# A causal convolution feeding a maxout layer: the band held still, the input moving, and DMA transposes in place of repack moves

## The chip, the cores and the metric

The kernel runs on one core of a Trainium2 chip. The metric is the device time of one execution in microseconds (us); it was measured three times before the change: 473.76, 473.94 and 474.82 us, median 473.94 us. The profile shown below is of one further execution, with a span of 472.8 us.

## The reference

The input `x` has 8 sequences of 4160 tokens with 192 channels. The channels form 8 heads of 24. Each head has a causal filter over 7 tokens, whose weights are a softmax. The 33280 filtered tokens go through a layer that takes the largest of three projections to 768 and projects that back to 192.

```python
w = exp(weight - max) / sum                      # 8 heads x 7 taps
x_pad = 6 zero tokens ahead of each sequence
y[b, s, h, :] = sum_k w[h, k] * x_pad[b, s + k, h, :]
h   = max(y @ w1, y @ w2, y @ w3)                # 192 -> 768
out = h @ w_out                                  # 768 -> 192, float32
```

The kernel uses max(a, b, c) = c + max(max(a - c, 0), b - c): it multiplies `y` by w1 - w3 and w2 - w3 and adds `y @ (w3 @ w_out)` at the end.

## The kernel before

The tokens are worked in 65 blocks of 512: 64 blocks out of the sequences, and one (block 58 in the order of work) of the last 64 tokens of all eight. A block goes through these parts:

- `load_x`: a DMA on SyncE's queue brings the tokens as float32, token by partition, in five chunks of 112 tokens that overlap by six and more.
- `cast_x`: GpSimd turns them into float16.
- `conv`: TensorE. A 112-by-32 piece of `x` is the stationary operand, a band matrix with the filter of one head is the moving one. The result in PSUM has channels as partitions and tokens as columns. As 24 channels don't fill 32 columns of the array, each head has a slot of 32.
- `evac`: ScalarE and VectorE copy the result to SBUF as float16.
- `repack`: six DMAs close the gaps between the slots, so that 64 channels lie in 64 partitions, three times (`yd`).
- `double`: one DMA copies the lower 64 partitions of `yd` to the upper 64, as TensorE works with two row groups of 64 at a time.
- `l1`: for each of six strips of 128 hidden units, TensorE computes the two differences into the PSUM tiles `lp` and `lq`; ScalarE takes max(lp, 0), VectorE the maximum with `lq`, to give `h`.
- `st2`: TensorE multiplies `h` by `w_out` and `y` by w3 @ w_out into `po`; ScalarE and VectorE add the two halves, and a DMA on GpSimd's queue stores the result.

The first four blocks have a convolution of their own (`conv_dense`), which the change leaves as it is.

```python
P, NBLK, HALF, PAD, GRP, NHEAD = 128, 512, 64, 6, 24, 8
SLOTS = ((0, 1, 2, 3), (6, 7, 4, 5))

def cast_x(t):
    ...
    for (rl, q0, q1) in parts:
        nc.gpsimd.tensor_copy(out=v[0:rl, q0:q1, :], in_=xf[0:rl, q0:q1, :])

def conv(t, pools=((psw, "w"), (psw, "w"))):
    G = [pool.tile([P, NBLK], FP32, ...) for i, (pool, tag) in enumerate(pools)]
    for (q, b, row_lo, rlen, lo, hi, cc) in chunks_of[t]:      # 5 chunks of up to 103 tokens
        for i in range(2):
            for g in range(4):
                h = SLOTS[i][g]
                cb = q * D + GRP * h + EDGE * (g % 2)
                nc.tensor.matmul(
                    G[i][32 * g:32 * g + 32, lo:hi],
                    lhsT=x16[0:rlen, cb:cb + 32],
                    rhs=band[0:rlen, h, cc:cc + hi - lo],
                    start=True, stop=True, tile_position=(0, 32 * g))

def evac(t, i, copy=nc.scalar.copy):
    copy(out=slots[t][:, i, :], in_=convs[t][i][:])

def repack(t):
    for n, (half, s0, c, r0, rows) in enumerate(pieces):       # 6 pieces
        (nc.sync, nc.gpsimd)[n % 2].dma_start(out=yd[r0:r0 + rows, c, :],
                                              in_=slots[t][s0:s0 + rows, half, :])

def double(t):
    nc.sync.dma_start(out=dense[t][HALF:P, :, :], in_=dense[t][0:HALF, :, :])

def make_m(i):                                                 # w3 @ w_out, once
    ...
            for e in range(2):
                nc.tensor.matmul(ps[HALF * e:HALF * (e + 1), :], lhsT=w3t[:, j, P:D],
                                 rhs=wo[:, j, :], start=(j == 0), stop=(j == NJ - 1))

def l1(t, j, pools=((psp, "p"), (psq, "q"))):
    for c in range(NC):                                        # 3
        for i in range(2):
            row = slice(HALF * i, HALF * (i + 1))
            nc.tensor.matmul(ps[i][:, 0:N], lhsT=wd[row, c, P * j:P * (j + 1)],
                             rhs=y[row, c, 0:N], start=(c == 0), stop=(c == NC - 1))
    nc.scalar.activation(out=r, in_=ps[0], func=AF.Relu)
    nc.vector.tensor_max(out=hs[t][:, j, 0:N], in0=r, in1=ps[1])
...
for t in range(2, NB):            # the steady state, t > 4
    load_x(t + 6)
    double(t + 2)
    cast_x(t + 5)
    l1(t, 0)
    if t % 2 == 0:                # the convolutions of two blocks together
        conv(t + 3); conv(t + 4)  # then evac: twice ScalarE, twice VectorE
    repack(t + 3)
    st2(t - 1, 0, NJ)
    for j in range(1, NJ):
        l1(t, j)
        st2(t - 1, j, NJ)
    store(t - 1)
```

Of the kernel before, what the change touches and what calls it, by code (L numbers as in the profile page):

```python
# [9 lines left out]
FP32 = mybir.dt.float32  # L10
FP16 = mybir.dt.float16
# [3 lines left out]
P = 128  # L15
KW = 7
PAD = KW - 1
NHEAD = 8
GRP = 24
BAND_W = 128 + PAD  # L20
NBLK = 512
CHK = 103
HALF = P // 2
# [4 lines left out]
def kernel(  # L28
# [12 lines left out]
    nc = tc.nc  # L41
    ctx.enter_context(tc.manual_schedule())

    B, SEQ, D = x.shape
# [6 lines left out]
    blocks = []  # L51
# [4 lines left out]
    segs, off = [], 0  # L56
# [25 lines left out]
                            o_lo - (row_lo - S)))  # L82
        return res

    chunks_of = [conv_chunks(blk) for blk in blocks]
    NQ = len(chunks_of[0])

    const = ctx.enter_context(tc.tile_pool(name="const", bufs=1))
    xap = ctx.enter_context(tc.tile_pool(name="xap", bufs=1))
    xbp = ctx.enter_context(tc.tile_pool(name="xbp", bufs=1))  # L90
    xfp = ctx.enter_context(tc.tile_pool(name="xfp", bufs=6))
    ysp = ctx.enter_context(tc.tile_pool(name="ysp", bufs=4))
    ydp = ctx.enter_context(tc.tile_pool(name="ydp", bufs=6))
    rp = ctx.enter_context(tc.tile_pool(name="rp", bufs=4))
    hp = ctx.enter_context(tc.tile_pool(name="hp", bufs=2))
# [4 lines left out]
    psq = ctx.enter_context(tc.tile_pool(name="psq", bufs=2, space=bass.MemoryType.PSUM))  # L100
    psw = ctx.enter_context(tc.tile_pool(name="psw", bufs=4, space=bass.MemoryType.PSUM))

    NDENSE = 4

    SLOTS = ((0, 1, 2, 3), (6, 7, 4, 5))
    EDGE = 32 - GRP
    xin = {}  # L110
    nlast = len(chunks_of[ENDS])
    x16s = [const.tile([P, NQ * D + 2 * EDGE], FP16, name=f"x16_{i}") for i in range(4)]
    x16z = const.tile([P, nlast * D + 2 * EDGE], FP16, name="x16_z")

    def load_x(t, eng=nc.sync):
        if not 0 <= t < NB:
            return
        chunks = chunks_of[t]
        n = len(chunks)
        pool, tag = (xfp, "xf") if t > 1 else ((xap, "xa"), (xbp, "xb"))[t]  # L120
        xf = (pool.tile([P, NQ, D], FP32, tag=tag, name=f"xf_{t}") if n <= NQ else
              const.tile([P, n, D], FP32, name=f"xf_{t}"))
        parts = []
        i, n = 0, len(chunks)
        row = [c[1] * SEQ + c[2] for c in chunks]
        while i < n:
            k = i
            while (k + 1 < n and chunks[k + 1][3] == chunks[i][3]
                   and row[k + 1] - row[k] == row[i + 1] - row[i]):
                k += 1  # L130
            step = row[i + 1] - row[i] if k > i else 0
            rlen = chunks[i][3]
            src = bass.AP(tensor=x.tensor, offset=row[i] * D,
                          ap=[[D, rlen], [step * D, k - i + 1], [1, D]])
            eng.dma_start(out=xf[0:rlen, i:k + 1, :], in_=src)
            if parts and parts[-1][0] == rlen:
                parts[-1] = (rlen, parts[-1][1], k + 1)
            else:
                parts.append((rlen, i, k + 1))
            i = k + 1  # L140
        xin[t] = [xf, None, parts]

    def cast_x(t):
        if not 0 <= t < NB:
            return
        xf, _, parts = xin[t]
        n = len(chunks_of[t])
        x16 = x16s[t % 4] if n <= NQ else x16z
        v = x16[:, EDGE:EDGE + n * D].rearrange("p (q d) -> p q d", d=D)
        for (rl, q0, q1) in parts:  # L150
            nc.gpsimd.tensor_copy(out=v[0:rl, q0:q1, :], in_=xf[0:rl, q0:q1, :])  # L151
        xin[t][1] = x16

    NC, NSLOT, CYC = D // HALF, D // 32, 96
    assert all(len(chunks_of[t]) == NQ for t in range(NDENSE))
    xz = {t: [const.tile([P, NQ, D], FP16, name=f"xz_{t}_{v}") for v in range(2)] for t in range(2)}
    xz[2], xz[3] = xz[0], xz[1]

# [38 lines left out]
    make_identity(nc, ident[:])  # L199
    ident16 = const.tile([P, P], FP16)  # L200
    nc.gpsimd.tensor_copy(out=ident16[:], in_=ident[:])
    for x16 in x16s + [x16z]:
        w = x16.shape[1] - EDGE
        nc.gpsimd.memset(x16[:, 0:EDGE], 0.0)
        nc.gpsimd.memset(x16[:, w:w + EDGE], 0.0)

    idle = const.tile([P, NBLK], FP16)
    nc.vector.memset(idle[:], 0.0)  # L208
    def keep_warm(n, pool=psw, tag="w"):
# [74 lines left out]
        nc.scalar.copy(out=m16[:, i, :], in_=ps[:])  # L284


    slots, dense, hs, outs, halves, convs, done = {}, {}, {}, {}, {}, {}, {}

    def conv(t, pools=((psw, "w"), (psw, "w"))):
        if t >= NB:  # L290
            return
        G = [pool.tile([P, NBLK], FP32, tag=tag, name=f"G{i}_{t}") for i, (pool, tag) in enumerate(pools)]
        x16 = xin[t][1]
        for (q, b, row_lo, rlen, lo, hi, cc) in chunks_of[t]:
            for i in range(2):
                for g in range(4):
                    h = SLOTS[i][g]
                    cb = q * D + GRP * h + EDGE * (g % 2)
                    nc.tensor.matmul(  # L299
                        G[i][32 * g:32 * g + 32, lo:hi],  # L300
                        lhsT=x16[0:rlen, cb:cb + 32],
                        rhs=band[0:rlen, h, cc:cc + hi - lo],
                        start=True, stop=True, tile_position=(0, 32 * g))
        slots[t] = ysp.tile([P, 2, NBLK], FP16, tag="ys", name=f"ys_{t}")
        convs[t] = G
        xin.pop(t)

    def conv_dense(t, copies):

# [31 lines left out]
    def evac(t, i, copy=nc.scalar.copy):  # L341
        if t >= NB:
            return
        copy(out=slots[t][:, i, :], in_=convs[t][i][:])  # L344


    pieces = ((0, 8, 0, 0, 48), (0, 72, 0, 48, 16), (0, 88, 1, 0, 32),
              (1, 72, 1, 32, 32), (1, 104, 2, 0, 16), (1, 8, 2, 16, 48))

    def repack(t):  # L350


        if t >= NB:
            return
        yd = dense[t] = ydp.tile([P, NC, NBLK], FP16, tag="yd", name=f"yd_{t}")
        for n, (half, s0, c, r0, rows) in enumerate(pieces):
            (nc.sync, nc.gpsimd)[n % 2].dma_start(out=yd[r0:r0 + rows, c, :],  # L357
                                                  in_=slots[t][s0:s0 + rows, half, :])

    def double(t):  # L360

        if NDENSE <= t < NB:
            nc.sync.dma_start(out=dense[t][HALF:P, :, :], in_=dense[t][0:HALF, :, :])

    def l1(t, j, pools=((psp, "p"), (psq, "q"))):


        N, y = blkN[t], dense[t]
        ps = [pool.tile([P, NBLK], FP32, tag=tag, name=f"l{tag}{i}_{t}_{j}")
              for i, (pool, tag) in enumerate(pools)]  # L370
        for c in range(NC):
            for i in range(2):
                row = slice(HALF * i, HALF * (i + 1))
                nc.tensor.matmul(ps[i][:, 0:N], lhsT=wd[row, c, P * j:P * (j + 1)],  # L374
                                 rhs=y[row, c, 0:N],
                                 start=(c == 0), stop=(c == NC - 1))
        r = rp.tile([P, NBLK], FP16, tag="r", name=f"r_{t}_{j}")
        nc.scalar.activation(out=r[:, 0:N], in_=ps[0][:, 0:N], func=AF.Relu)  # L378
        nc.vector.tensor_max(out=hs[t][:, j, 0:N], in0=r[:, 0:N], in1=ps[1][:, 0:N])  # L379

    def st2(t, u, NU):
# [2 lines left out]

        if t < 0:
            return
        hT, y = hs[t], dense[t]
        if u == 0:
            todo = [[], []]
            for s in range(4):  # L390
                tok = slice(P * s, P * (s + 1))
                for i in range(2):
                    row = slice(HALF * i, HALF * (i + 1))
                    mm = [(y[row, i, tok], m16[row, 0, :])]
                    if s % 2 == i:
                        mm.append((y[row, 2, tok], m16[row, 1, :]))
                    hh = [(hT[row, j, P * s:P * (s + 1)], wo[row, j, :]) for j in range(NJ)]
                    mm = hh + mm if t == 0 else mm + hh
                    todo[i] += [(s, n == 0, n == len(mm) - 1, m) for n, m in enumerate(mm)]
            if t == NB - 1:  # L400

                for i in range(2):
                    k = [sum(e[0] < s for e in todo[i]) for s in range(5)]
                    lot = [todo[i][k[s]:k[s + 1]] for s in range(4)]
                    todo[i] = lot[0][:-1] + lot[1][:-1] + lot[0][-1:] + lot[1][-1:] + lot[2] + lot[3]
            halves[t] = (todo, {})
# [99 lines left out]

    convs_at = {2: (4,), 3: (5, 6)}
    doubles_at = {2: (), 3: (4,), 4: (5, 6)}  # L510
    for t in range(2, NB):
        if t > 4:
# [9 lines left out]
        if t == 2:  # L522
            conv_dense(3, (nc.scalar.copy, nc.vector.tensor_copy, nc.scalar.copy))
            cross_dma(3)
            load_x(7)
        us = convs_at.get(t, (t + 3, t + 4) if t % 2 == 0 else ())
        for n, u in enumerate(us):
            conv(u, PQ if n or t == 2 else ((psw, "w"), (psw, "w")))
        for u in us:
            evac(u, 0)  # L530
        for u in us[::-1]:
            evac(u, 1, nc.vector.tensor_copy)
        if t == 2:
            repack(4)
            load_x(8)
            cast_x(5)
            cast_x(6)
        elif t == 3:
            repack(5)
            repack(6)  # L540
            load_x(9)
            cast_x(7)
            cast_x(8)
        else:
            repack(t + 3)
        st2(t - 1, 0, NJ)
        for j in range(1, NJ):
            l1(t, j)
# [37 lines left out]
```

The softmax here doesn't subtract the row's maximum and nothing guards it: scores larger than these inputs give would overflow.

## Time and profile before

| What | Before |
|---|---|
| time, median of three | 473.94 us |
| span of the profile | 472.8 us |
| TensorE matmul busy | 466.7 us (99%) |
| VectorE busy | 367.8 us (78%) |
| ScalarE busy | 325.5 us (69%) |
| GpSimd busy | 217.1 us (46%) |
| matmuls of the convolution (line 299) | 2400 of 112x103 and 64 of the block of sequence ends |
| evacuation of the convolution (line 344) | 61 of 588 ns on ScalarE, 61 of 683 ns on VectorE |
| bytes moved by DMA | 81.49 MB, on average 172 GB/s |

In the profile PE is TensorE's matmul, PEld its loading of stationary operands, DVE VectorE, ACT ScalarE, POOL GpSimd and SP SyncE; an engine's name with a q is its queue of instructions, where DMAs are issued. L299 is a line of the kernel. A row of the timeline gives the start in us, the length in us, the engine, the line, the operation, "output <- inputs", the shape of the array, the operand's size, and how many instructions of the kind followed one another; then, in brackets, how long the engine had been idle and what ended that. In the forty slices each digit is a share in tenths. A row of the waits says who waited for whom, then the microseconds in all, how often, and the longest.

### The profile page before, as it was taken

What the parts mean: (1) busy time and instruction counts of PE and PEld (TensorE: products, weight loads), DVE (VectorE), ACT (ScalarE), POOL (GpSimd) and SP (SyncE); (2) the same over time, 40 slices, a digit from 0 to 9 for tenths busy, and PEclk for the clock granted to TensorE, in tenths of its full rate; (3) what the DMA queues carried; (4) which work ended last, traced back from release to release, by engine and by line L of the source; (5) the groups of instructions that cost most, each with busy time, mean ns of one, the idle gap of its engine ahead of it and who ended that gap; (6) DMA issues with size and microseconds to landing.
All of it is one profiled execution on the core that took longest, in us unless ns stands there. A gap on an engine that the chain in (4) does not pass through costs nothing.

```text
span 472.8 us, 21832 instructions
## 1 busy us (share of the span) xinstructions
PE 466.7 (99%) x9033; PEld 391.3 (83%) x9033; DVE 367.8 (78%) x607; ACT 325.5 (69%) x609; POOL 217.1 (46%) x352
## 2 busy tenths in 40 slices
PE   8999999999999999999999999999999999999996
PEld 4487888888888888888888888888888888888996
DVE  6878777777777787787877877778778787787775
ACT  5767767667666676676766766677677666776664
POOL 6745555355445445354534543543553454454210
PEclk9999999999999999999999999999999999999999
DMA  8947877666676666667566666656665765664423
GB/s 198 255 112 184 210 200 200 171 171 177 168 197 170 176 177 176 161 190 205 156 171 181 183 162 195 190 142 192 172 187 166 199 174 152 183 191 103 109 85 103
DMA packets 68258, 81.49 MB, mean 172 GB/s; under 512 B 9311, under 2 KB 57247, under 8 KB 68159
## 3 DMA queue, kind: packets, MB, share of 16 engines
q1 hardware_dynamic: 55070, 49.21, 42.0%
q0 software_dynamic: 12928, 30.78, 21.3%
q8 instruction: 71, 1.16, 1.1%
q14 instruction: 29, 0.23, 0.2%
q10 hardware_dynamic: 160, 0.10, 0.1%
HBM read 30.31 MB, written 25.56 MB: 118 GB/s over the span
## 4 chain that ended last, share of the span: by engine, by line
PE 96%; DVE 2%; DMA 1%; issue 1%; ACT 0%; SPq 0%; DVEq 0%
PE lp L374 32%; PE po L418 30%; PE lq L374 26%; PE G L299 7%; DMA xf<-in_x_dram 1%; PE D L318 1%; DVE xz L170 1%; PE lw L374 0%; DVE yd L334 0%; DVE h L379 0%; DVE wd L254 0%; PE pm L282 0%; PE pm L278 0%; ACT yd L327 0%; ACT yd L324 0%
## 5 line engine op out<-in xcount | busy, mean ns | idle before, releaser
L379 DVE TENSOR_TENSOR h<-r,lq 128x512 f16<-128x512 f16 x386 | 264.7, 686 | 96.7 <-ACT r L378 96.6
L378 ACT ACTIVATE r<-lp 128x512 f16<-128x512 f32 x386 | 230.5, 597 | 133.5 <-PE lp L374 88.5
L374 PE MATMUL lp<-yd,wd 64*128 64x512 f16 x1158 | 312.2, 376 | 0.8 <-DVE wd L254 0.6
L374 PE MATMUL lq<-yd,wd 64*128 64x512 f16 x1158 | 311.9, 375 | 0.3 <-DVE yd L334 0.3
L418 PE MATMUL po<-wo,h 64*128 64x192 f16 x3120 | 230.4, 243 | 0.0
L418 PEld LDWEIGHTS <-h 64*128 64x128 f16 x3120 | 186.4, 94 | 25.7
L374 PEld LDWEIGHTS <-wd 64*128 64x128 f16 x2340 | 163.9, 94 | 23.2 <-issue 2.9
L447 POOL DMA_DIRECT2D out_dram<-o x64 | 51.3, 802 | 235.6 <-DVE o L428 223.7
L357 POOL DMA_DIRECT2D yd<-ys x183 | 92.4, 511 | 1.4 <-ACT ys L344 0.8
L418 PE MATMUL po<-m,yd 64*128 64x192 f16 x780 | 87.0, 243 | 0.0
L428 DVE TENSOR_TENSOR o<-a,po 128x384 f32<-128x384 f32 (+1 forms) x132 | 71.4, 542 | 1.0 <-ACT a L427 1.0
L427 ACT COPY a<-po 128x384 f32<-128x384 f32 (+1 forms) x132 | 61.7, 468 | 2.1 <-PE po L418 2.1
L418 PEld LDWEIGHTS <-yd 64*128 64x128 f16 x780 | 54.9, 94 | 8.0
L151 POOL CAST x<-xf 112x960 f16<-112x960 f32 x60 | 59.6, 996 | 1.7 <-PE lq L374 1.6
L344 DVE CAST ys<-G 128x512 f16<-128x512 f32 x61 | 39.2, 683 | 0.0
L299 PEld LDWEIGHTS <-x 112*32 112x32 f16 x2400 | 28.6, 96 | 12.7 <-issue 12.3
L344 ACT CAST ys<-G 128x512 f16<-128x512 f32 x61 | 33.0, 588 | 1.3
L299 PE MATMUL G<-band,x 112*32 112x103 f16 (+1 forms) x2400 | 33.3, 209 | 0.0
L213 PE MATMUL idle<-idle 128*128 128x512 f16 x15 | 6.3, 564 | 1.2 <-DVE idle L208 1.2
L170 POOL CAST xz<-xf 112x80 f16<-112x80 f32 (+2 forms) x18 | 5.2, 334 | 3.3 <-DMA xf<-in_x_dram 2.8
L318 PEld LDWEIGHTS <-xz 112*32 112x32 f16 x240 | 4.3, 104 | 2.3 <-issue 1.4
L318 PE MATMUL D<-band,xz 112*32 112x103 f16 (+1 forms) x240 | 5.1, 223 | 0.1
(52 smaller groups left out, 57.7 us busy)
## 6 DMA issues: line engine op xcount, KB each, us to landing
xf<-in_x_dram SPq DMA_DIRECT2D x57, 420.0 KB, 4.7
out_dram<-o POOLq DMA_DIRECT2D x62, 384.0 KB, 4.2
yd<-yd SPq DMA_DIRECT2D x61, 192.0 KB, 3.1
yd<-ys POOLq DMA_DIRECT2D x61, 48.0 KB, 3.4
yd<-ys SPq DMA_DIRECT2D x61, 48.0 KB, 3.9
xf<-in_x_dram SPq DMA_DIRECT2D x8, 252.0 KB, 4.0
yd<-ys POOLq DMA_DIRECT2D x61, 32.0 KB, 3.4
yd<-ys SPq DMA_DIRECT2D x61, 32.0 KB, 3.3
```

The source lines that it names most:

```text
L151: nc.gpsimd.tensor_copy(out=v[0:rl, q0:q1, :], in_=xf[0:rl, q0:q1, :])
L299: nc.tensor.matmul(G[i][32 * g:32 * g + 32, lo:hi], lhsT=x16[0:rlen, cb:cb + 32], rhs=band[0:rlen, h, cc:cc + hi - lo], start=True, stop=T ...
L318: nc.tensor.matmul(ps[32 * g:32 * g + 32, lo:hi], lhsT=xz[t][v][0:rlen, q, 32 * s:32 * s + 32], rhs=band[0:rlen, h, cc:cc + hi - lo], star ...
L344: copy(out=slots[t][:, i, :], in_=convs[t][i][:])
L357: (nc.sync, nc.gpsimd)[n % 2].dma_start(out=yd[r0:r0 + rows, c, :], in_=slots[t][s0:s0 + rows, half, :])
L374: nc.tensor.matmul(ps[i][:, 0:N], lhsT=wd[row, c, P * j:P * (j + 1)], rhs=y[row, c, 0:N], start=(c == 0), stop=(c == NC - 1))
L378: nc.scalar.activation(out=r[:, 0:N], in_=ps[0][:, 0:N], func=AF.Relu)
L379: nc.vector.tensor_max(out=hs[t][:, j, 0:N], in0=r[:, 0:N], in1=ps[1][:, 0:N])
L418: nc.tensor.matmul(ps[b0, i][:, s % 2, :], lhsT=a, rhs=b, start=first, stop=last)
L427: nc.scalar.copy(out=a[:, ss, :], in_=ps[s0, 0][:, ss, :])
L428: nc.vector.tensor_add(out=outs[t][:, s0:s + 1, :], in0=a[:, ss, :], in1=ps[s0, 1][:, ss, :])
L447: qs[0].dma_start(out=bass.AP(tensor=out.tensor, offset=r * D, ap=[[D, n], [step * D, s1 - s0], [1, D]]), in_=ob[p0:p0 + n, s0:s1, :])
```

## The change

From block 4 on the roles of the operands are exchanged. The band of one head, 70 rows (64 tokens and six ahead of them) by 64 columns, becomes the stationary operand, and `x` moves. The blocks are cut into eight rows of 64 tokens with the six tokens ahead of each; the odd and the even ones go to the two column halves of the array, and two blocks are worked with the same stationary operand. The result has tokens as partitions and channels as columns, without gaps. As the layers need channels as partitions, a DMA transpose (`turn`) turns each block, 128 x 768 float16, into `yd`. Its six 128 x 128 pieces put the 64-channel groups by turns in the lower and the upper partitions, and `double` exchanges the two halves with two DMAs into a second set. `l1` and `st2` pick the groups from there by `spot`. The repack moves and the 32-wide slots go away.

```diff
     def cast_x(t):
...
-        for (rl, q0, q1) in parts:
-            nc.gpsimd.tensor_copy(out=v[0:rl, q0:q1, :], in_=xf[0:rl, q0:q1, :])
+        if u == 0:
+            x16s[t0] = x16p.tile([P, NHEAD, 2, nu, NR // 2, GRP], FP16, tag="x16", name=f"x16_{t0}")
+        if p0:
+            nc.gpsimd.memset(xf[0:p0, 0, :], 0.0)
+        K = HALF + PAD
+        for c in range(2):
+            nc.gpsimd.tensor_copy(out=x16s[t0][0:K, :, c, u, :, :].rearrange("p h r c -> p r h c"),
+                                  in_=xf[0:K, c:NR:2, :].rearrange("p r (h c) -> p r h c", c=GRP))
...
-    def conv(t, pools=((psw, "w"), (psw, "w"))):
+    def conv(t, pools):
...
+        w = nu * (NR // 2) * GRP
+        G = [pool.tile([P, per, w], FP32, tag=tag, name=f"G{i}_{t}") for i, (pool, tag) in enumerate(pools)]
+        for h in range(NHEAD):
+            for c in range(2):
+                nc.tensor.matmul(
+                    G[h // per][HALF * c:HALF * (c + 1), h % per, :],
+                    lhsT=band[0:HALF + PAD, h, PAD:HALF + PAD],
+                    rhs=x16s[t0][0:HALF + PAD, h, c, :, :, :].rearrange("p u r c -> p (u r c)"),
+                    start=True, stop=True, tile_position=(0, HALF * c))
...
-        copy(out=slots[t][:, i, :], in_=convs[t][i][:])
+        copy(out=slots[t][:, :, :, GRP * per * i:GRP * per * (i + 1)].rearrange(
+                 "p u r (h c) -> p h (u r) c", c=GRP),
+             in_=G[i][:].rearrange("p h (n c) -> p h n c", c=GRP))
...
-    def repack(t):
+    def turn(t):
...
-        for n, (half, s0, c, r0, rows) in enumerate(pieces):
-            (nc.sync, nc.gpsimd)[n % 2].dma_start(out=yd[r0:r0 + rows, c, :],
-                                                  in_=slots[t][s0:s0 + rows, half, :])
+        t0, u, nu = place(t)
+        yd = dense[t] = ydp.tile([P, 2, NCH // 2, P], FP16, tag="yd", name=f"yd_{t}")
+        nc.sync.dma_start_transpose(out=yd[:, 0, :, :],
+                                    in_=slots[t0][:, u, :, :].rearrange("p r d -> p (r d)"))

     def double(t):

         if NDENSE <= t < NB:
-            nc.sync.dma_start(out=dense[t][HALF:P, :, :], in_=dense[t][0:HALF, :, :])
+            yd = dense[t]
+            for i in range(2):
+                nc.sync.dma_start(out=yd[HALF * i:HALF * (i + 1), 1, :, :],
+                                  in_=yd[HALF * (1 - i):HALF * (2 - i), 0, :, :])
...
     def l1(t, j, pools=((psp, "p"), (psq, "q"))):
...
-                                 rhs=y[row, c, 0:N],
+                                 rhs=y_all(t, i, c),
...
-        us = convs_at.get(t, (t + 3, t + 4) if t % 2 == 0 else ())
...
+        u = convs_at.get(t, t + 3 if t % 2 == 0 else NB)
+        conv(u, PQ if t == 2 else WW + PQ)
...
-            repack(t + 3)
+            turn(t + 3)
```

`y_all` names the four runs of 128 tokens of one 64-channel group, and `y_tok`, in `st2`, one of them. The pools change with it: three buffers for the float16 input of a pair of blocks, three for the evacuated pairs.

## The prediction

> **What bounds the kernel now.** I first read the busy totals and the forty slices of the profile page.
>
> ```profile
> PE 466.7 (99%) x9033; PEld 391.3 (83%) x9033; DVE 367.8 (78%) x607; ACT 325.5 (69%) x609; POOL 217.1 (46%) x352
> ...
> PE   8999999999999999999999999999999999999996
> ...
> PEclk9999999999999999999999999999999999999999
> DMA  8947877666676666667566666656665765664423
> ```
>
> TensorE is busy in every slice at an undiminished clock; VectorE has about a fifth of its time free, ScalarE three tenths, GpSimd half, the DMA engines about a third. Busy time alone proves nothing for pipelined matmuls, so the chain of work that ended last comes next.
>
> ```profile
> PE 96%; DVE 2%; DMA 1%; issue 1%; ACT 0%; SPq 0%; DVEq 0%
> PE lp L374 32%; PE po L418 30%; PE lq L374 26%; PE G L299 7%; DMA xf<-in_x_dram 1%; PE D L318 1%; DVE xz L170 1%; PE lw L374 0%; DVE yd L334 0%; DVE h L379 0%; DVE wd L254 0%; PE pm L282 0%; PE pm L278 0%; ACT yd L327 0%; ACT yd L324 0%
> ```
>
> 96% of the end is TensorE's own stream. What the change rewrites is the part G (line 299), 7%: about 33 us. Everything it does to other engines is worth nothing unless it starts to delay that stream. Next, the matmul timeline around one convolution of two blocks.
>
> ```profile
> 210.54 0.38 PE L374 MATMUL lp<-yd,wd 64*128 64x512 f16 x1
> 210.63 0.38 PE L374 MATMUL lq<-yd,wd 64*128 64x512 f16 x1
> 210.94 0.95 PEld L299 LDWEIGHTS <-x 112*32 112x32 f16 x80 [0.42 <-issue]
> 210.94 1.10 PE L299 MATMUL G<-band,x 112*32 112x103 f16 x80
> ...
> 211.97 0.33 PE L418 MATMUL po<-m,yd 64*128 64x192 f16 x3
> ```
>
> 80 matmuls start within 1.10 - 0.21 = 0.89 us (0.21 is the length of one), so one every 11.3 ns. 103 columns at 2.4 per ns are 42.9 ns; four column groups running side by side make 10.7 ns. So the four groups do overlap, and the stage streams at almost its column count; weight loads keep up. The convolution before this one started at 196.99 us, so two blocks take 13.95 us. Twelve steps of layer work at 1.06 us (the matmul timeline repeats at that distance) are 12.72; the convolution with the drains on both sides is the other 1.23.
>
> **What the Trainium skill says.** "TensorEngine Tiling (Array Packing)", section Tiling Modes, says that column tiles work in parallel and that a change of mode drains the array. The trace agrees with both: 11.3 ns per matmul above, and the 0.42 us for which the weight loader sat before line 299. For two column groups of 64 the trace has its own instance, make_m(1):
>
> ```profile
> 21.66 0.69 PE L282 MATMUL pm<-wo,w3t 128*64 128x192 f16 x12
> ```
>
> Twelve matmuls of 192 columns start within 0.69 - 0.246 = 0.44 us, one every 40 ns, half of 192/2.4 = 80 ns. That is the very form of the new convolution. For the transposes no row of this trace helps. "DMA: Bandwidth & Descriptors", section Latency and other measured facts, gives a DMA transpose 261 GB/s with a non-contiguous middle dimension; its section on the X-bar says such a transpose must be issued from SyncE or ScalarE. "VectorE: DVE Perf Modes", section The three transpose paths, gives 1309 ns for one 128x128 of 2-byte numbers. No run shows either figure yet.
>
> **The change, part by part.**
>
> (1) The convolution on TensorE. Before: 80 matmuls per pair of blocks, 80 x 11.3 = 904 ns. After: 8 heads x 2 halves = 16 matmuls of 2 x 4 x 24 = 192 columns, at 40.9 ns (the measured pace, taken as 0.44 or 0.45 over 11 intervals) 655 ns. The column arithmetic agrees: 2 x 512 x 8 / 4 = 2048 columns before, 8 x 192 = 1536 after, 0.213 us at 2.4 per ns. I take 0.25 us a pair. Both have two changes of mode, so I keep the drains. There are 30 pairs and one single block: 30 x 0.25 = 7.5 us, the single one about 0.1. The contraction gets shorter too (112 rows to 70), which I count as nothing: rows of the array work at once. **Sum: -7.5 us.**
>
> (2) The layers. The moving operand of line 374 becomes four runs of 128 columns, the stationary one of line 418 is still 128 dense columns. Same counts, same columns: 0.
>
> (3) Evacuation. Two copies of 128x512 on each of ScalarE (588 ns) and VectorE (683 ns) per pair become two of 128x384 each. ScalarE's row for 128x384 is 468 ns, VectorE's by proportion about 550. That is 0.24 and 0.27 us less per pair on engines that do not set the end: 0.
>
> (4) The cast on GpSimd. One of 112x960 (996 ns) becomes two of 70x768. The trace has one of 70x1536 at 1477 ns, so about 1.5 us, somewhat more for 24-number runs. The three DMA issues of 511 ns leave the engine at the same time. GpSimd comes out even, with half its time free: 0. In the opening stage the casts of blocks 5 and 6 took 32.1 to 34.0 us and their convolution began at 35.97; longer casts still fit because the issues ahead of them are gone. I allow +0.4 us for the opening.
>
> (5) The DMAs. The loads and the doubling move the same bytes (420 and 192 KB). The six repack moves, 192 KB a block, become one transpose of 192 KB. Moves of that size are 61 x 0.197 = 12 of the 81.5 MB, so by bytes some 15% of a DMA share of about 0.65: 0.65 us of a 6.95 us block. At 261 GB/s the transpose takes 0.75 us. The DMA engines stay at about two thirds.
>
> (6) The order on SyncE's queue. The waits of that queue show what the repack costs in latency now:
>
> ```profile
> SPq L363 <- DMA yd<-ys: 170.1, 103, 5.7
> SPq L357 <- ACT r L378: 23.6, 31, 2.1
> ```
>
> 170 us over 61 blocks: 2.8 us of each block the queue stands before the doubling until the repack has landed. It will do the same for the transpose. Let L be the time from the transpose's issue to its landing. In a pair: evacuation, transpose (L), two doubling issues (2 x 0.5 us), the second transpose (L), two doubling issues, next evacuation. That is 2L + 2 us in 13.95, so the queue keeps up while L is under about 6 us. My estimate of L: 0.75 us of moving, 1.3 us that even a single 128x128 needs by the page, and latency as in the doubling (3.1 us to landing for the same bytes): 3.5 to 4 us. A block's doubling is issued nearly two blocks before its first use, so even 5 us delays no matmul. Cost: 0.
>
> Sum: 473.9 - 7.5 + 0.4 = **466.8 us**, 1.5% less.
>
> **Rivals.**
>
> A. *The transpose is slow and its queue becomes the bound.* For it: nothing in the trace has timed one, transposes share the engines with two thirds of other traffic, and every block's doubling waits on one. Against: the page's rates, and about two blocks of slack. If L were 8 us, a pair would take 2 x 8 + 2 = 18 us and the kernel 30 x 4 = 120 us more, near 590. I give L over 6 us, or a queue held for that long, one chance in eight.
>
> B. *The drains are part of the saving.* The convolution costs 1.23 us of which only 0.90 is streaming. If part of the 0.33 around it comes from the 80 small instructions and the four groups, 16 larger ones give some of it back; saving another 0.1 us a pair makes 463.5, faster by over 2%. For it: with fewer instructions there is less to queue. Against: the mode changes stay, and make_m's 12 matmuls also took 0.61 us from their first start to the next work, 0.17 beyond the 0.44. One chance in five.
>
> C. *Side effects eat the gain.* 24-number runs could slow the casts or evacuations. GpSimd would have to lose 3 us per block to bound the kernel, VectorE 1.5. A late evacuation would hold a PSUM buffer that line 374 wants two steps later. That would make 470 to 475, the same within 2%. Some of the middle belongs to it.
>
> **Range and chances.** The centre is 466.8. The 2% mark below is 464.5, only 2.3 us away, so B counts: faster 0.20. Above it is 483.4, which only A reaches, or a bad C: slower 0.16. Within 2%: 0.64. Range 462 to 479.
>
> **What would show it.** (1) right: the new G row has 16 matmuls per pair in about 0.65 us between first and last start, plus one length; G is about 5% of the chain; pair distance near 13.7 us. (3), (4) right: evacuations of 128x384 near 470 and 550 ns, casts below 1 us each. (5) right: DMA digits still mostly 6 and 7. (6) right: the wait of the doubling on the transpose no longer than about 4 us a block, and no idle of TensorE before line 374 that a doubling ends. The prediction is wrong if the two column groups do not overlap (16 x 80 ns = 1.28 us, about 478 us), if the transpose takes over 6 us to land, or if TensorE starts to wait for yd.

## The result, and the profile after

The changed kernel takes 467.89 us (median of four, 467.19 to 468.07) against 474.38 us before (median of four in the same comparison). The ratio is 0.9855, with a 95% interval of 0.9839 to 0.9871: faster by 1.5%. The predicted time was 466.8 us.

The page of the changed kernel first (span 466.3 us): busy totals, three rows of the forty slices, the two large DMA queues, and the chain that ended last.

```profile
PE 460.1 (99%) x7065; PEld 385.6 (83%) x7065; DVE 359.6 (77%) x607; ACT 317.0 (68%) x609; POOL 162.7 (35%) x227
...
PE   8899999999999999999999999999999999999996
...
PEclk9999999999999999999999999999999999999999
DMA  8958997778687777878777768767686976784512
...
q1 hardware_dynamic: 99804, 55.17, 57.6%
q0 software_dynamic: 7072, 24.78, 14.8%
...
PE 95%; DMA 2%; SPq 2%; POOL 0%; issue 0%; DVE 0%; ACT 0%
PE lq L399 34%; PE po L442 33%; PE lp L399 22%; PE G L301 5%; DMA wos<-in_moe_w_out_dram 2%; SPq L190 1%; PE D L319 0%; SPq L134 0%; POOL wo L515 0%; PE pm L280 0%; PE pm L284 0%; DVE o L452 0%; ACT a L451 0%
```

The array still sets the end and is still busy in every slice; the convolution G went from 7% of the chain to 5%. What changed visibly is what lies off the path: GpSimd fell from 46% to 35%, the DMA engines rose. By the sum of their packets' times the two queues together took 63.3% of the DMA engines' time before (42.0 and 21.3) and take 72.4% now, for the same 80 MB.

The groups that the prediction named follow, out of the page's costliest groups.

```profile
L158 POOL CAST x<-xf 70x768 f16<-70x768 f32 x122 | 97.4, 833 | 3.0 <-DMA xf<-in_x_dram 2.6
...
L347 DVE CAST ys<-G 128x384 f16<-128x384 f32 x61 | 31.0, 550 | 0.0
L347 ACT CAST ys<-G 128x384 f16<-128x384 f32 x61 | 26.2, 485 | 0.0
L301 PE MATMUL G<-x,band 70*64 70x192 f16 (+1 forms) x496 | 26.1, 248 | 0.0
```

The evacuations take 485 and 550 ns and the casts 833 ns each. Now the timeline around one convolution of the changed kernel, on all engines, weight loads left out.

```profile
207.83 0.38 PE L399 MATMUL lq<-yd,wd 64*128 64x512 f16 x1
208.06 0.60 ACT L403 ACTIVATE r<-lp 128x512 f16<-128x512 f32 x1
...
208.13 0.85 PE L301 MATMUL G<-x,band 70*64 70x192 f16 x16
208.24 0.55 DVE L452 TENSOR_TENSOR o<-a,po 128x384 f32<-128x384 f32 x1
...
208.70 0.68 DVE L404 TENSOR_TENSOR h<-r,lq 128x512 f16<-128x512 f16 x1
...
208.92 0.34 PE L442 MATMUL po<-m,yd 64*128 64x192 f16 x3
...
209.34 0.38 PE L399 MATMUL lp<-yd,wd 64*128 64x512 f16 x1
209.44 0.37 PE L399 MATMUL lq<-yd,wd 64*128 64x512 f16 x1
```

From the first matmul of G to the first of the next work (po) it is 0.784 us (208.132 to 208.916 in the trace). Before it was 1.034. In the 28 pairs of whole blocks the two numbers repeat within 5 ns: 0.250 us saved. The 16 matmuls start within 0.605 us. After them lp and lq start 0.10 us apart here, and 0.18 us apart after the next convolution (221.83):

```profile
222.48 0.68 DVE L404 TENSOR_TENSOR h<-r,lq 128x512 f16<-128x512 f16 x1
...
223.04 0.38 PE L399 MATMUL lp<-yd,wd 64*128 64x512 f16 x1
...
223.22 0.37 PE L399 MATMUL lq<-yd,wd 64*128 64x512 f16 x1
```

Before the change they started together, 0.13 us after VectorE's maximum (h) had ended. These rows belong to the convolution at 210.94 that the prediction shows:

```profile
211.59 0.68 DVE L379 TENSOR_TENSOR h<-r,lq 128x512 f16<-128x512 f16 x1
...
212.39 0.38 PE L374 MATMUL lp<-yd,wd 64*128 64x512 f16 x1
212.40 0.38 PE L374 MATMUL lq<-yd,wd 64*128 64x512 f16 x1
```

What this costs comes out below.

The distance from one pair to the next was 13.95 us throughout, but for 14.04 us once, at the block of sequence ends. Now it takes two values by turns, as the matmul timeline shows:

```profile
194.35 0.85 PE L301 MATMUL G<-x,band 70*64 70x192 f16 x16
...
208.13 0.85 PE L301 MATMUL G<-x,band 70*64 70x192 f16 x16
...
221.83 0.85 PE L301 MATMUL G<-x,band 70*64 70x192 f16 x16
```

13.78 and 13.70 us. So of each two pairs one keeps the whole 0.25 us and the other 0.17.

Last, the queue of SyncE, with the transposes (line 358), the loads (134) and the doublings (366):

```profile
210.39 1.25 SPq L358 DMA_TRANSPOSE yd<-ys  x1
211.74 0.50 SPq L134 DMA_DIRECT2D xf<-in_x_dram  x1
212.97 1.11 SPq L366 DMA_DIRECT2D yd<-yd  x2
214.13 1.30 SPq L358 DMA_TRANSPOSE yd<-ys  x1
215.53 1.42 SPq L134 DMA_DIRECT2D xf<-in_x_dram  x1
218.74 1.10 SPq L366 DMA_DIRECT2D yd<-yd  x2
```

The doubling at 212.97 had to wait for the transpose of 210.39: 2.6 us from its issue to its landing. For the transpose of 214.13 it is 4.6 us. In the steady part these times go from 2.5 to 5.3 us, with a median of 3.3.

### The profile page after: what moved, and what is told of

Read it like the earlier page. It is cut to its first block, busy times and chain, and to the rows that moved or that the text cites. A ratio compares the mean times of both kernels' runs of the same rounds, so it can differ in the third digit from the quotient of the medians.

```text
span 466.3 us, 17191 instructions
## 1 busy us (share of the span) xinstructions
PE 460.1 (99%) x7065; PEld 385.6 (83%) x7065; DVE 359.6 (77%) x607; ACT 317.0 (68%) x609; POOL 162.7 (35%) x227
## 3 DMA queue, kind: packets, MB, share of 16 engines
q1 hardware_dynamic: 99804, 55.17, 57.6%
## 4 chain that ended last, share of the span: by engine, by line
PE 95%; DMA 2%; SPq 2%; POOL 0%; issue 0%; DVE 0%; ACT 0%
PE lq L399 34%; PE po L442 33%; PE lp L399 22%; PE G L301 5%; DMA wos<-in_moe_w_out_dram 2%; SPq L190 1%; PE D L319 0%; SPq L134 0%; POOL wo L515 0%; PE pm L280 0%; PE pm L284 0%; DVE o L452 0%; ACT a L451 0%
## 5 line engine op out<-in xcount | busy, mean ns | idle before, releaser
L442 PE MATMUL po<-wo,h 64*128 64x192 f16 x3120 | 248.9, 243 | 0.0
L442 PEld LDWEIGHTS <-h 64*128 64x128 f16 x3120 | 203.6, 94 | 17.4
L471 POOL DMA_DIRECT2D out_dram<-o x64 | 48.1, 752 | 281.4 <-DVE o L452 215.0
L158 POOL CAST x<-xf 70x768 f16<-70x768 f32 x122 | 97.4, 833 | 3.0 <-DMA xf<-in_x_dram 2.6
L442 PE MATMUL po<-m,yd 64*128 64x192 f16 x780 | 95.7, 243 | 0.0
L347 DVE CAST ys<-G 128x384 f16<-128x384 f32 x61 | 31.0, 550 | 0.0
L301 PEld LDWEIGHTS <-band 70*64 70x64 f16 x496 | 19.5, 109 | 12.8 <-PE lp L399 12.7
L347 ACT CAST ys<-G 128x384 f16<-128x384 f32 x61 | 26.2, 485 | 0.0
L301 PE MATMUL G<-x,band 70*64 70x192 f16 (+1 forms) x496 | 26.1, 248 | 0.0
L335 DVE COPY yd<-yd 64x512 f16<-64x512 f16 x9 | 4.3, 474 | 1.0 <-ACT yd L328 0.5
```

Source lines behind the costliest of these rows:

```text
L158: nc.gpsimd.tensor_copy(out=x16s[t0][0:K, :, c, u, :, :].rearrange("p h r c -> p r h c"), in_=xf[0:K, c:NR:2, :].rearrange("p r (h c) -> p ...
L301: nc.tensor.matmul(G[h // per][HALF * c:HALF * (c + 1), h % per, :], lhsT=band[0:HALF + PAD, h, PAD:HALF + PAD], rhs=x16s[t0][0:HALF + PAD ...
L347: copy(out=slots[t][:, :, :, GRP * per * i:GRP * per * (i + 1)].rearrange("p u r (h c) -> p h (u r) c", c=GRP), in_=G[i][:].rearrange("p h ...
L442: nc.tensor.matmul(ps[b0, i][:, s % 2, :], lhsT=a, rhs=b, start=first, stop=last)
L471: qs[0].dma_start(out=bass.AP(tensor=out.tensor, offset=r * D, ap=[[D, n], [step * D, s1 - s0], [1, D]]), in_=ob[p0:p0 + n, s0:s1, :])
```

## The experiments

All start from the changed kernel. Spans are of the profiled execution (466.3 us for the changed kernel), and a pair's distance is from one convolution's first matmul to the next one's. A ratio is to the kernel before, with its 95% interval.

### The convolution twice

Theory: the time is TensorE's columns. Rival: the gain came from the shorter evacuations and the issues taken off GpSimd.

```diff
-        for h in range(NHEAD):
+        for h in [k for k in range(NHEAD) for _ in range(2)]:
```

> Every convolution matmul of the changed kernel is issued twice, 32 for 16 per pair, each writing the same numbers again. Theory (the time is TensorE's columns, and the convolution's share of them is what the change cut): 16 more matmuls at 0.041 us are 0.66 us a pair, 30 pairs and one single block give about 20 us, less the 1 us of small waits before the maximum's operand that the longer stage hides: 485 to 486 us in the profile against 466.3. Rival (the gain came from the shorter evacuations and the DMA issues taken off GpSimd, TensorE has room): under 8 us more.

Measured: span 484.5 us, 486.32 us median, ratio 1.0241 (1.0215 to 1.0268). From G to po it is 1.444 us, 0.660 more, which is what 16 more matmuls at 0.041 us make. Pairs are at 14.36 us without turns, 0.62 above the mean of 13.70 and 13.78. TensorE has no room at this place. That other engines had no part in the gain follows from the timeline and not from this run alone: the whole saving lies between G and po. The span came out 0.5 us under the expected range.

### The same columns in twice as many matmuls

```diff
-            for c in range(2):
-                nc.tensor.matmul(G[...][..., h % per, :], ..., rhs=x16s[t0][0:K, h, c, :, :, :])
+            for u in range(nu):
+                for c in range(2):
+                    nc.tensor.matmul(G[...][..., h % per, 96 * u:96 * (u + 1)], ..., rhs=x16s[t0][0:K, h, c, u, :, :])
```

> The pair's matmuls of 192 columns become two of 96 columns each, 32 instructions for the same columns. Theory (columns only): 466 to 467 us, the stage still 0.78 us from its first matmul to the next work. Rival (fewer, larger instructions are part of the gain, a start costs something beside its columns): at 10 ns a start 16 more make 0.16 us a pair, 471 us, at more accordingly.

Measured: span 466.1 us, ratio 0.9851 (0.9828 to 0.9874), from G to po 0.803 us for 0.784. Sixteen more instructions add 0.02 us, where the rival's 10 ns each would have added 0.16. So rival B of the prediction, by which fewer and larger instructions would give more, falls for this form. The four column groups of the old form are not tested here, but the traces speak on them: from the last lq start to G it is 0.306 us in both kernels, and beyond its streaming the stage cost 0.33 us before and costs 0.32 now.

### Plain copies in place of the transposes

The turning is left out here; the same 192 KB are moved.

```diff
-        nc.sync.dma_start_transpose(out=yd[:, 0, :, :],
-                                    in_=slots[t0][:, u, :, :].rearrange("p r d -> p (r d)"))
+        nc.sync.dma_start(out=yd[:, 0, :, :].rearrange("p k q -> p (k q)"),
+                          in_=slots[t0][:, u, :, :].rearrange("p r d -> p (r d)"))
```

> The DMA transpose becomes a plain DMA copy of the same 192 KB, so the turning is left out and the output is not the reference's. Theory (the transpose is hidden): the same time within 1 us, though the DMA engines' share falls from about 0.73 to 0.65 and SyncE's queue waits less. Rival (the transpose delays the stream somewhere, by its place on the queue or by crowding the loads): more than 1 us faster.

Measured: span 465.7 us, ratio 0.9850 (0.9822 to 0.9878), with the same 13.70 and 13.78 by turns. The transposes cost the end nothing. The page shows what they cost the DMA engines (packets, MB, share of the 16 engines):

```profile
q1 hardware_dynamic: 59788, 55.17, 44.7%
q0 software_dynamic: 7072, 24.78, 14.2%
```

The same bytes, but 57.6% of the engines' time falls to 44.7% on SyncE's queue, and the DMA share of the whole span from 0.73 to 0.60, more than expected. Each transpose is 768 packets of 256 bytes at 31.6 ns, 1.52 us of all 16 engines; the plain copy's 128 packets of 1536 bytes take about 0.6 us (what the packets of that size take more than in the changed kernel, over 61 blocks). From issue to landing the plain copy takes 2.7 us in the median, the transpose 3.3.

### Two and three transposes for one

```diff
+        for _ in range(1):                       # range(2) for three
+            xt = xtp.tile([P, NCH // 2, P], FP16, tag="xt", name="xt")
+            nc.sync.dma_start_transpose(out=xt[:], in_=slots[t0][:, u, :, :].rearrange("p r d -> p (r d)"))
```

> Every DMA transpose is issued twice, the second time into a tile that nobody reads. Theory (hidden, with room): in the trace one transpose is 768 packets of 256 bytes at 31.6 ns, 1.52 us of all 16 engines, so their load goes from 5.0 to 6.6 us of a 6.87 us block: still the same time within 1.5 us, DMA share about 0.95 of the steady part. Rival (it was just hidden: the queue, or loads that come later through crowding, bind): 5 us or more slower.

> Every DMA transpose three times, two of them into a tile that nobody reads. By the same count the DMA engines would need 5.0 + 3.0 = 8.1 us of a 6.87 us block, so now they bind: 61 x 1.2 = 75 us slower, about 540 us, with TensorE waiting. Rival (packets of transposes overlap with others, the measured times of packets are not time used up): under 500 us.

Measured with two: 469.13 us median, ratio 0.9895 (0.9861 to 0.9929). The seven times go from 468.38 to 473.66 us, and the profiled one, with a span of 471.9 us, is the longest of them. By the median the theory holds: 1.2 us above the changed kernel. In the steady part nothing changes, 13.70 and 13.78 us by turns, though the packets' times add up to 1.04 of the DMA engines' time from 60 to 400 us. The 5.6 us of the profiled execution were lost at one place in the opening:

```profile
45.12 0.60 PE L404 MATMUL lp<-yd,wd 64*128 64x512 f16 x1 [2.16 <-DMA yd<-yd]
...
45.52 0.63 PE L404 MATMUL lp<-yd,wd 64*128 64x512 f16 x1
```

TensorE waited 2.16 us for a doubling. Then it worked at a granted clock of 0.50 from 45.0 to 51.8 us (0.63 us for a matmul that takes 0.38 elsewhere), which is another 3.4 us. The queue was behind there: between 32 and 51 us the transposes and doublings of several blocks follow one another on it. Why the clock fell is not shown.

Measured with three: 503.43 us in a single execution, span 501.7 us. Its DMA row and its waits of TensorE's weight loads, with the reason after the arrow:

```profile
DMA  8969999999999999999999999999999999999962
...
PEld L404 <- DMA yd<-yd: 27.1, 29, 3.1
```

and its queue of SyncE, where L359 and L363 are the transposes:

```profile
313.42 2.76 SPq L359 DMA_TRANSPOSE yd<-ys  x1
316.27 2.56 SPq L363 DMA_TRANSPOSE xt<-ys  x2
318.89 0.56 SPq L135 DMA_DIRECT2D xf<-in_x_dram  x1
319.49 1.11 SPq L371 DMA_DIRECT2D yd<-yd  x2
320.71 2.60 SPq L359 DMA_TRANSPOSE yd<-ys  x1
```

Now the layers wait for the doublings, and from the fourth convolution on pairs are 13.7 to 16.6 us apart. It came to 35 us and not 75. The packets' times add up to 1.13 of the DMA engines' time from 60 to 400 us, which is more than there is. So the rival's reason holds, that these times are not all time used up, although the result lies 1.7 us above its 500. That the DMA engines bind is not shown either: SyncE's queue is as full. One issue follows the other there, and the issues fill 92% of the time from 60 to 400 us (45% in the changed kernel, 69% with two transposes). There 28 of 136 transposes hold the queue for over 2 us (1 of 49 in the changed kernel), so the engines may be what delays it. Which of the two comes first stays open.

### The convolution in two stages

The 13.70 us of a pair are 12 steps of 1.06 us and 0.98 us more, of which 0.66 is streaming. What is the rest? I took it for drains.

```diff
-        conv(u, WW + PQ)
+        conv(u, WW + PQ, range(4))        # heads 0 to 3
...
         for j in range(1, NJ):
             l1(t, j)
+            if late and j == 1:
+                conv(u, WW + PQ, range(4, 8)); evac(u, 2); evac(u, 3, nc.vector.tensor_copy)
```

> The convolution is cut in two: heads 0 to 3 where it was, heads 4 to 7 after the second strip of the layer, so that the array goes through four changes of mode per pair and not two. The columns are the same. Theory (of the 0.98 us that a pair pays for its convolution 0.66 is streaming and 0.32 belongs to the drains of the two mode changes): 0.25 to 0.33 us more a pair, 474 to 476 us. Rival (the 0.32 us is a wait of that place, for a PSUM buffer or an operand): about 466 to 469 us.

Measured: span 490.5 us, ratio 1.0363 (1.0341 to 1.0385), 0.84 us more a pair. Both expectations missed, because the edit brought a wait of its own: the second stage takes its lp and lq buffers after l1(t, 1), so that l1(t, 2) gets the ones that l1(t, 1) has just filled:

```profile
206.03 0.69 DVE L407 TENSOR_TENSOR h<-r,lq 128x512 f16<-128x512 f16 x1 [0.81 <-ACT r L406]
...
206.23 0.38 PE L402 MATMUL lp<-yd,wd 64*128 64x512 f16 x1
...
206.77 0.37 PE L402 MATMUL lq<-yd,wd 64*128 64x512 f16 x1 [0.16 <-DVE h L407]
```

lq starts 0.54 us after lp, when VectorE's maximum has ended. The next edit keeps the order of the buffers.

```diff
         conv(u, WW + PQ, range(4))
         st2(t - 1, 0, NJ)
+        conv(u, WW + PQ, range(4, 8)); evac(u, 2); evac(u, 3, nc.vector.tensor_copy)
```

> The convolution is cut in two once more, but so that the PSUM buffers keep their order: heads 0 to 3 where they were, then the five matmuls per row group of the output layer that followed anyway, then heads 4 to 7. Theory (a pair of mode changes costs the 0.32 us that the stage takes beyond its 0.66 us of streaming): 0.27 to 0.33 us more a pair, of which the 0.04 us of waits for the maximum are given back, 29 pairs: 473 to 475 us in the profile. Rival (changes of mode are nearly free, and most of what the first split cost, and of the 0.32, is waiting): under 470 us.

Measured: span 480.5 us, ratio 1.0148 (1.0112 to 1.0185), pairs at 14.24 us, 0.54 above 13.70. Again more than expected, and again most of it is a wait that the split brought:

```profile
213.71 0.52 PE L304 MATMUL G<-x,band 70*64 70x192 f16 x8
...
213.90 0.55 DVE L455 TENSOR_TENSOR o<-a,po 128x384 f32<-128x384 f32 x1
214.16 0.59 PE L445 MATMUL po<-m,yd 64*128 64x192 f16 x3
```

The three po matmuls take 0.59 us for 0.34 in the changed kernel. By the trace the first row group starts at 214.162 and the second at 214.497: it needs the PSUM buffer that VectorE's addition sets free, which ends at 214.443, 0.054 us before. The same distance lies between the maximum and lq in the next two sections. That is 0.335 of the 0.54 us; 0.2 are left for a pair of mode changes. The changed kernel agrees: from its last lq start to G it is 0.306 us, 0.09 more than the 0.216 between matmuls of that line, and from the last G to po 0.179, 0.10 more than the 0.083 between two G of one column group.

### The first maximum in halves

```diff
+        cuts = (0, N // 2, N) if j == 0 and t > 3 and t % 2 == 0 else (0, N)
+        for a, b in zip(cuts, cuts[1:]):
+            nc.scalar.activation(out=r[:, a:b], in_=ps[0][:, a:b], func=AF.Relu)
+            nc.vector.tensor_max(out=hs[t][:, j, a:b], in0=r[:, a:b], in1=ps[1][:, a:b])
```

> In the blocks with a convolution the first strip's relu and maximum are done in two halves of 256 columns, so that the maximum ends, and its PSUM buffer comes free, about 0.1 us earlier. Theory (in every second pair lq starts 0.08 us late after the convolution because this maximum ends late, and that lag is lost at the next change of mode): all pairs 13.70 us instead of 13.70 and 13.78 by turns, 15 x 0.08 = 1.2 us less, 465.1 us in the profile. Rival (the turns of 13.70 and 13.78 come from something that alternates by itself, as the buffers do): unchanged, 466.3 us.

Measured: span 466.8 us, ratio 0.9868 (0.9836 to 0.9899), and all pairs at 13.78 us. So neither: the turns are gone, which speaks for a cause in this maximum, but all pairs have the slower value. The two halves did not end earlier. VectorE's rows of this kernel:

```profile
208.06 0.55 DVE L454 TENSOR_TENSOR o<-a,po 128x384 f32<-128x384 f32 x1
208.52 0.74 DVE L406 TENSOR_TENSOR h<-r,lq 128x256 f16<-128x256 f16 x2
```

The halves begin only when the output's addition ahead of them is nearly done, and together last 0.74 us for 0.68. They end 1.315 us after the convolution's start, where the whole one ended after 1.252 and 1.330 by turns. lq starts 0.054 to 0.057 us after the end in all three cases (1.372, 1.306, 1.384). In these kernels lq follows the end of the maximum, whenever that is.

### Half of the convolution left out

```diff
-        for h in range(NHEAD):
+        for h in range(0, NHEAD, 2):      # and the evacuation copies each computed head twice
```

> Half of the convolution is left out: of each two heads that share a PSUM bank only the first is computed, 8 matmuls for 16 per pair, and the evacuation copies it twice; all other work is as in the changed kernel, the output is not the reference's. Rival (TensorE's columns set the time here, as they did for the change): 8 x 0.041 = 0.33 us a pair, 30 pairs, 10 us less, 456 to 457 us in the profile. Theory (the change has brought this stage to the next limit: after a convolution the layer's lq waits for VectorE's maximum, which ends 1.25 us after the convolution's start with VectorE busy without a break before it, and the output layer's second row group waits for VectorE's addition, which ends 0.73 us after that start): lq can't start before 1.30 us, where it starts already, so at most 0.1 us a pair, 463.5 to 466.5 us.

Measured: span 464.4 us, 465.94 us median, ratio 0.9812 (0.9796 to 0.9829), pairs at 13.68 us. Half the columns of the convolution, 0.33 us a pair, bring 0.06 us, as the theory said. The timeline of this kernel around a convolution:

```profile
207.35 0.52 PE L301 MATMUL G<-x,band 70*64 70x192 f16 x8
207.43 0.55 DVE L454 TENSOR_TENSOR o<-a,po 128x384 f32<-128x384 f32 x1
...
207.80 0.49 PE L444 MATMUL po<-m,yd 64*128 64x192 f16 x3
207.90 0.68 DVE L406 TENSOR_TENSOR h<-r,lq 128x512 f16<-128x512 f16 x1
...
208.38 0.38 PE L401 MATMUL lp<-yd,wd 64*128 64x512 f16 x1
...
208.63 0.37 PE L401 MATMUL lq<-yd,wd 64*128 64x512 f16 x1
```

lq starts 1.284 us after the convolution's start, 0.053 after the maximum's end at 1.231; in the changed kernel it was 1.306 or 1.384. The array looks busy all the same (98% of the span), as lp runs ahead alone in its row group.

## Why the prediction was right, point by point

**(1) The convolution, -7.5 us.** The mechanism and the size per pair were right: 0.250 us by the trace, 0.25 predicted from the pace of make_m and of line 299. The convolution issued twice confirms the slope (0.660 us for 16 more matmuls), and the 96-column run that the columns count and hardly the instructions. That the shorter contraction is worth nothing is right too: 70 rows give one matmul every 40.3 ns, make_m's 128 rows one every 40. One sum in the signs of being wrong is off: 16 x 80 ns = 1.28 us would have made about 485 us and not 478, and the convolution issued twice, of just that length, had a span of 484.5.

**What the step missed** is that 0.08 us of it is given back in every second pair. Between the regular pairs the mean saving is 0.211 us, not 0.25; 14 times 0.078 is 1.1 us. After a convolution l1(t, 1) needs the lq buffer of l1(t, 0), which VectorE's maximum empties 1.25 to 1.33 us after the convolution's start. Before the change that was 1.33, and lq was not wanted until 1.458 us; now it would be at 1.21. So lq's row group falls behind lp's by 0.10 or 0.18 us, stays behind for the two blocks, and at the next change of mode the group ahead has to wait. A lag of 0.10 us is no loss against before, as the groups were 0.095 us apart then too when a convolution began; the 0.08 us beyond it is. When it lags by 0.18, lp ended early, so relu and maximum begin early, and after that convolution the lag is 0.10; with 0.10 it is the other way round. Hence the turns. Three kernels with different ends of the maximum (changed, halved maximum, half convolution) all have lq 0.053 to 0.057 us after it. I had counted nothing for this; the rival C named a buffer held by a late evacuation, but it is the buffer of the maximum, and the evacuations became faster.

**The sum.** Predicted were 7.1 us less, measured are 6.5 (467.89 for 474.38). From the first regular convolution to the last it is 5.98 us, the opening brought 0.29 and the end 0.22. That the total came so close is in part luck: the 1.1 us that step (1) missed and the 0.7 us by which the opening came out better than allowed for have opposite signs.

**(2) The layers, 0.** Right: their matmuls have the durations of before, 376 and 243 ns, and the steps repeat at 1.06 us.

**(3), (4) Evacuation and casts, 0.** Right in size (485 and 550 ns, though 683 ns by proportion would be 512; 833 ns twice, a little above the 1.5 us) and in having no effect. But GpSimd did not come out even: 0.7 us more of casts and 1.5 us less of issues a block take it from 217.1 to 162.7 us, as step (4)'s own numbers would have said. The +0.4 us for the opening did not come: the first regular pair starts at 43.27 us, before at 43.56.

**(5) The DMA engines.** The path's cost of 0 was right, the load was wrong: I expected two thirds still, and it is 76% in the steady part (66% before; that a block is 6.98 us and not 6.95 changes nothing). The Trainium skill's "DMA: Bandwidth & Descriptors" (Latency and other measured facts) gives a transpose 261 GB/s; here 192 KB in 1.52 us of packet time are 130 GB/s. The measured packet time is what foretells the share here. It is no rate of a transpose by itself, which no run shows: with three transposes packet times add up to more than all of the engines' time.

**(6) The queue.** Right in the outcome: 2.5 to 5.3 us from issue to landing in the steady part, median 3.3, against an estimate of 3.5 to 4, all below the 6 us at which the queue would bind, and no wait of TensorE for the turned tile. The estimate was not the sum of its terms, as 0.75 + 1.3 + 3.1 is 5.15 us. Doubling the transposes left the steady part untouched.

**Rivals.** A did not occur; with three transposes a block the layers do wait, with the queue of SyncE and the DMA engines both full. B fell with the 96-column run and with the same 0.3 us beside the streaming in both kernels (its 463.5 us should read 463.8). Of these 0.32 us about 0.2 are drains, and about 0.1 is the lag between the row groups when the convolution begins.

Open is what a drain costs by itself, as both splits brought a wait of their own; the 0.2 us are what is left after such waits.

## What to carry to other kernels

When TensorE sets the time, count the columns each form streams, with the number of column groups that run side by side, and take the pace from a row of the same form; that is what the change can be worth at this place. Then look for what the shortened stage ran beside: a buffer that came free shortly before it was wanted (0.13 us here) becomes the wait after, and the row of that engine tells how much can be had. Here leaving out half of the convolution's remaining columns brought a fifth of their time, though the array shows 99%.

## What was not expected of the hardware

- A DMA transpose of 128x768 float16 from SBUF to SBUF is 768 packets of 256 bytes, 1.52 us of packet time on all 16 engines, some 2.6 times a plain copy of the same bytes, and holds its issuing queue for 1.29 us in the median.
- The packets' times can add up to more than the engines have: 1.04 of their time with two transposes a block, without a loss in the steady part, and 1.13 with three. A DMA digit of 9 is no proof of a bound.
- The two row groups of the array can be apart for a long time: in the changed kernel they keep 0.10 or 0.17 us over the 12 steps between two convolutions. It costs time only where a change of mode makes them meet.
- In the profiled executions with two and three transposes, a wait of TensorE of 2.16 and of 2.92 us in the opening was followed by 6.8 and 3.4 us at half the granted clock. In the first of them that cost more than the wait itself.
